# A hinted jump over a guard, first tokens read ahead of weights, and later tables, in a kernel of two attention and two gated layers

## The chip, the core and the metric

The kernel runs on one NeuronCore of a Trainium2 chip. The core has five engines, each with a queue of instructions of its own that it works off in order: TensorE (PE) multiplies matrices, VectorE (DVE), ScalarE (ACT) and GpSimd (POOL) work on rows of numbers, and SyncE (SP) mostly issues transfers (DMAs). They wait for one another through semaphores. On-chip data lie in a buffer of 128 partitions; products are summed in eight banks of a second memory, PSUM. The metric is the device time of one execution in microseconds (us), as a median of several runs; lower is better.

## What is computed

A residual stream x of 2048 tokens with 448 features goes through attention, a gated MLP, the same attention and the same MLP again, with a layer norm ahead of each. The attention has 16 heads of 28 features and no mask.

```python
B, S, D, H = 1, 2048, 448, 16            # F = 1792
def _A_ref(x, wqkv, wo):
    qkv = (x @ wqkv).reshape(B, S, 3, H, Dh).transpose(2, 0, 3, 1, 4)
    q, k, v = qkv[0], qkv[1], qkv[2]
    p = softmax(einsum("bhqd,bhkd->bhqk", q, k) * Dh ** -0.5)
    o = einsum("bhqk,bhkd->bhqd", p, v)
    return o.transpose(0, 2, 1, 3).reshape(B, S, D) @ wo
def _B_ref(x, w_gate, w_up, w_down):
    return (sigmoid(x @ w_gate) * (x @ w_up)) @ w_down

x = x + _A_ref(layernorm(x), A_wqkv, A_wo)
x = x + _B_ref(layernorm(x), B_w_gate, B_w_up, B_w_down)
x = x + _A_ref(layernorm(x), A_wqkv, A_wo)
x = x + _B_ref(layernorm(x), B_w_gate, B_w_up, B_w_down)
```

All of it is in float32. The kernel keeps that accuracy with half-precision products: a number is split into a high and a low float16 part, and three products (high by high, high by low, low by high) stand for one.

## The kernel before

**Order.** The program is written out by hand and not rescheduled: each engine runs its instructions in the order in which the Python code issues them. Each layer has four stages: `project` (q, k and v of all tokens), `attend`, `out_project`, `gated`. Tokens go in four blocks of 512 (`NB`), a block in four tiles of 128 (`TB`).

**The start (L1409 to L1444).** SP issues the reads: `wq.read(0)`, the 448 columns of q's weights (three transfers in `load_rows`: 384 rows, and the last 64 rows twice), then the first four token tiles, one transfer each, then k's weights, the next four tiles, v's weights, the other eight tiles. PE runs fourteen products on zeros (`keep_busy`, L243), which compute nothing that is used, to keep its clock up. ACT adds up the squares of the weights (`measure`, L541); PE sums them over partitions (`size`, L546); DVE makes a power of two of the sum (`powers`, L228 and L230); ACT writes the high half of the scaled weights (`high_cols`, L213) and DVE the low half (`low_cols`, L216). For the tokens, DVE takes the statistics of a tile (`stats`, L430 and L431), POOL makes one over the root of the variance (L433, L435), DVE scales the tile (`scale`, L278), PE turns it (`turn`, L443), and ACT and DVE copy it out of PSUM as high and low parts (`turned_high` L461, `turned_low` L468). POOL's first instructions build constants, among them `ind`, a table of ones that adds up the features of a head, whose last cast DVE makes (L182), and the rows of units that it writes to memory (`unit_scr`).

**`project` (L614).** `qk(b, blk, fill, before)` makes seven tiles of 128 columns of q and k for a block: eleven products each (`by_features`, L492), then ACT copies the high part and squares it (L658, L661), DVE makes the low part and a maximum (L659, L663), and SP writes both to memory (L666). Three tiles later PE adds the squares up for each head (L637, L640, into `qnorm` and `knorm`). In the first block the steps of `along` stand between the tiles and prepare the weights that come later: `measure(1)`, `size(1)`, the halves of k's weights, `measure(2)`, `size(2)`, and v's two halves. `fill[i]` is done behind tile i: for the first block the statistics of the second block's tiles (`b1.norm`) and their scaling (`scaled`). `vals(b, ...)` makes a block's values tile by tile, eleven products of 448 columns each (L514 to L519), and does `after[j]` behind the products of tile j; `fin`, returned by `qk`, adds up the last three tiles' squares and takes their maximum.

**The guard (L796).** The norms bound every score. `worst_of_heads` makes a flag of the bound, each engine loads it into a register (L795), and `tc.If(loose > 0)` runs `true_maxima` for all 16 heads where the bound is too loose: 1,040 products and as many weight loads for PE, in each layer. With these inputs the flag is 0 and every engine jumps over that code. Behind the jump stand the transfers of the first heads' operands and guard rows, the values of the last block's third tile, and the attention.

**`attend` (L1004).** A unit is a block of 128 keys by 512 queries of a head: 1,024 units in a layer. PE makes its scores (L1032), ACT takes the exponential of three units at a time (L1047), PE multiplies them with the values (L1083). Some units are set aside (`ASIDE`): their exponential is made on DVE, in ten instructions (`score_aside`, L1049 to L1067). `FEW` says how many a head sets aside in layer 0; it has 14 characters, and heads beyond it take two; in layer 1 every head takes three. Along with layer 0's attention, DVE and POOL prepare the other weights (`Prepare`). `finish` (L1112) ends a head with a transpose of its sum on DVE.

## Time and profile before

| what | value |
|---|---|
| median of 3 runs | 1936.16 us (1935.15 to 1939.42) |
| the profiled execution | 1937.4 us, span 1935.5 us |
| TensorE busy | 1919.4 us |
| ScalarE busy | 1313.4 us |
| VectorE busy | 1237.3 us |
| GpSimd busy | 164.3 us |
| mean granted TensorE clock | 0.998 |

The span runs from the first to the last instruction of the execution. In it layer 0 has its projection until about 119 us, its attention until 579, its output projection and MLP until about 990; layer 1 has the same with attention from 1080 to 1531. "Busy" counts the time in which an engine has an instruction at work; a product at half clock counts as busy for as long as it lasts. In a timeline each line has the start, the duration, the engine, the line of the code and the operation; behind it, in brackets, how long the engine was idle before it and what released it. The suffix "q" on an engine (PEq) means its sequencer, which fetches and issues the instructions. In the table of windows, each engine's busy time has its count of instructions behind it; then come the granted clock (1.00 is full), the share of the transfer engines' time, and GB/s.

### The profile page before, as it was taken

The page shows a single profiled execution, that of the slowest core. Times are in us where ns is not written, and L with a number is a line of the kernel's source. Part 1 is how long each engine was busy: PE and PEld are TensorE (multiplying, and loading weights), DVE is VectorE, ACT ScalarE, POOL GpSimd, SP SyncE. Part 2 cuts the span into 40 slices and gives each one's busy share as a digit, 9 for nine tenths or more (in the row PEclk, how much of TensorE's full clock was granted, in tenths as well). Part 3 has the DMA queues.
Part 4 walks back from the last instruction along what each step waited for, and adds up shares of the span by engine and source line. Part 5 has one row for each costly group of instructions (what it writes and reads, how often), then busy time and mean ns, then how long its engine had stood idle before and what let it go on. Part 6 is the DMA issues. An engine that isn't in the chain of part 4 may idle for free. (4 is left out here: it accounts for less than half of the span.)

```text
span 1935.5 us, 53590 instructions
## 1 busy us (share of the span) xinstructions
PE 1919.4 (99%) x23405; PEld 1240.8 (64%) x23405; DVE 1237.3 (64%) x2329; ACT 1313.4 (68%) x1573; POOL 164.3 (8%) x307
## 2 busy tenths in 40 slices
PE   9999999999999999999999999999999999999999
PEld 4445555555556777777754576666655577777776
DVE  7638878788655555555574477787778664655543
ACT  5559999999993343443445799999999644343432
POOL 2013322211001000000000000000000000000000
PEclk9999999999999999999999999999999999999999
DMA  5565664424216313242344321122111243333310
GB/s 172 162 203 151 186 199 123 123 84 130 63 62 242 107 69 107 71 132 81 99 117 131 94 51 37 40 51 51 38 39 65 100 171 117 107 111 103 111 46 20
DMA packets 90519, 201.53 MB, mean 104 GB/s; under 512 B 10814, under 2 KB 58014, under 8 KB 90144
## 3 DMA queue, kind: packets, MB, share of 16 engines
q1 hardware_dynamic: 65664, 111.02, 19.4%
q0 software_dynamic: 17776, 83.51, 13.0%
q8 instruction: 188, 3.08, 0.7%
q10 hardware_dynamic: 6832, 3.44, 0.6%
q14 instruction: 59, 0.48, 0.1%
HBM read 142.61 MB, written 47.98 MB: 98 GB/s over the span
## 5 line engine op out<-in xcount | busy, mean ns | idle before, releaser
L1047 ACT ACTIVATE prob_s<-sc 128x1536 f32<-128x1536 f32 x659 | 890.7, 1495 | 13.9 <-PE sc L1032 10.0
L1083 PE MATMUL acc<-prob_s,val_s 128*32 128x256 f32 (+3 forms) x7748 | 569.8, 383 | 0.0
L1032 PE MATMUL sc<-qp_s 114*32 114x512 f16 x7896 | 554.4, 379 | 3.2 <-issue 2.2
L507 PEld LDWEIGHTS <-gu_s 128*128 128x128 f16 x4368 | 426.8, 98 | 61.1 <-issue 1.3
L1032 PEld LDWEIGHTS <-qp_s 114*32 114x32 f16 x8192 | 268.8, 96 | 214.9 <-issue 101.1
L1083 PEld LDWEIGHTS acc<-prob_s,val_s 128*32 128x32 f32 x7748 | 272.0, 110 | 143.6 <-issue 12.0
L1336 DVE TENSOR_TENSOR one_q<-side,one_q 128x512 f32<-128x512 f32 x112 | 71.9, 683 | 298.4 <-PE side L507 298.4
L507 PE MATMUL chain<-xwide_s,gu_s 128*128 128x256 f16 x2016 | 247.6, 273 | 0.6 <-ACT one_q L1320 0.5
L1320 ACT COPY one_q<-chain 128x256 f32<-128x256 f32 x224 | 82.9, 372 | 205.9 <-PE chain L507 199.1
L1063 DVE SCALAR_TENSOR_TENSOR power_q<-power_q,expo_q 128x512 f32<-128x512 f32 x222 | 153.6, 692 | 7.6
L1289 PE MATMUL dnp<-dn_s,hhl_q 128*128 128x448 f16 x448 | 158.0, 353 | 0.0
L1290 PE MATMUL dnp<-dn_s,hhl_q 128*128 128x448 f16 x448 | 158.0, 353 | 0.0
L1291 PE MATMUL dnp<-dn_s,hhl_q 128*128 128x448 f16 x448 | 158.0, 353 | 0.0
L507 PE MATMUL side<-xshort_s,gu_s 128*128 128x256 f16 x1120 | 141.0, 273 | 0.0
L492 PE MATMUL qkp<-xhl_s,wqk_s 128*128 128x512 f16 x616 | 138.0, 379 | 0.8 <-DVE wqk_s L216 0.7
L1112 DVE STREAM_TRANSPOSE oturned_q<-acc 128x512 f32<-128x512 f32 x32 | 22.9, 716 | 143.5 <-PE acc L1083 143.4
L492 PEld LDWEIGHTS <-wqk_s 128*128 128x128 f16 x616 | 60.1, 98 | 70.4 <-DVE wqk_s L216 1.2
L507 PE MATMUL side<-xwide_s,gu_s 128*128 128x256 f16 x672 | 91.7, 273 | 0.0
L1320 ACT COPY two_q<-chain 128x256 f32<-128x256 f32 x112 | 41.7, 372 | 67.5 <-PE chain L507 67.5
L1083 PE MATMUL acc<-power_q,val_s 128*32 128x128 f32 (+3 forms) x276 | 86.3, 394 | 0.0
L1347 ACT ACTIVATE one_q<-one_q 128x512 f32<-128x512 f32 x56 | 35.3, 630 | 59.4 <-DVE one_q L1336 59.4
L1057 DVE TENSOR_SCALAR expo_q<-aside,base 128x512 f32<-128x512 f32 x74 | 55.4, 748 | 30.8 <-PE aside L1032 30.5
(186 smaller groups left out, 2076.7 us busy)
## 6 DMA issues: line engine op xcount, KB each, us to landing
gu_s<-gu_parts POOLq DMA_DIRECT2D x56, 800.0 KB, 4.8
qp_s<-qk_scr SPq DMA_DIRECT2D x96, 224.0 KB
gu_s<-gu_parts SPq DMA_DIRECT2D x20, 800.0 KB
qk_scr<-qkhl_q SPq DMA_DIRECT2D x56, 256.0 KB
gu_parts<-pack_s POOLq DMA_DIRECT2D x14, 800.0 KB, 3.8
xraw_s<-xt_scr SPq DMA_DIRECT2D x12, 768.0 KB
xt_scr<-xs_s SPq DMA_DIRECT2D x34, 224.0 KB
qp_s<-qk_scr SPq DMA_DIRECT2D x64, 112.0 KB
```

Of the source, the lines that this page charges most:

```text
L492: nc.tensor.matmul(pm, w, x, start=(i == 0), stop=(i == len(terms) - 1))
L507: nc.tensor.matmul(pm, a, x, start=(first and i == 0), stop=(i == len(terms) - 1), skip_group_check=True)
L1032: nc.tensor.matmul(ps[32 * j:32 * j + 32, :], hd.k[:, keys], hd.q[:, qb * W:(qb + 1) * W], start=True, stop=True, tile_position=(0, 32 * j))
L1047: nc.scalar.activation(prob[:, 0:n, :], ps[:, 0:n, :], AF.Exp, scale=exp_scale)
L1057: nc.vector.tensor_scalar(y, ps, base2[:, 0:1], -126.0, op0=ALU.mult, op1=ALU.max)
L1063: nc.vector.scalar_tensor_tensor(p, p, c[k], y, op0=ALU.add, op1=ALU.mult)
L1083: nc.tensor.matmul(acc[qb * VC:(qb + 1) * VC, s], v[:, kc % TB, h, :], probs[c * NB + qb][:, s], start=(kc == 0 and a == 0), stop=(kc == N ...
L1289: nc.tensor.matmul(pm, hl[:, 0, s], dw[:, 0, :], start=begin, stop=False)
L1290: nc.tensor.matmul(pm, hl[:, 0, s], dw[:, 1, :], start=False, stop=False)
L1291: nc.tensor.matmul(pm, hl[:, 1, s], dw[:, 0, :], start=False, stop=end)
L1320: nc.scalar.copy(to, pm)
L1336: nc.vector.tensor_tensor(one[m], side[m], one[m], op=ALU.add)
```

## The change

Four things are changed.

1. A hint on PE, "likely taken", is given for the branch of the guard: for layer 0 as the program's first PE instruction, for layer 1 in a new else block of layer 0's guard. In the built program each is one instruction of PE, `BranchPrefetchHint`.
2. At the start the four token tiles are read ahead of q's weights, whose rows come in four transfers instead of three, and whose squares are added up in two parts. Eight products on zeros instead of fourteen are made, and one fewer between the tiles. The sum of squares is taken behind the scaling of the fourth tile, and the larger high part of q's weights (columns 128 to 448) behind the copies of the turned tokens.
3. POOL's table `ind` and the unit rows are made after the first block's statistics, with the cast on POOL instead of DVE. The second block's statistics are taken behind tiles 2 and 3 instead of 0 and 2, its scaling behind tile 5 instead of 4, and in layer 0 `fin` of the second block is done behind the third value tile instead of the second.
4. `FEW` gets two characters more: heads 14 and 15 of layer 0 set three units aside instead of two.

```diff
@@ -61,7 +61,7 @@
 
 
 ASIDE = {1: ((6, 15, 1),), 2: ((4, 10, 3), (9, 15, 1)), 3: ((4, 9, 3), (8, 13, 1), (12, 15, 2))}
-FEW = "22211212121212"
+FEW = "2221121212121233"
 
 N_SLOTS = 19
 N_QUART = 12
@@ -149,6 +149,7 @@
 
     ones = cpool.tile([P, P], F32, name="ones")
     sums = cpool.tile([P, 7], F32, name="sums")
+    rest = cpool.tile([P, 1], F32, name="rest")
     size = cpool.tile([P, 7], F32, name="size")
     pw = cpool.tile([P, 7], I32, name="pw")
     up = cpool.tile([P, 7], F32, name="up")
@@ -168,30 +169,34 @@
     nc.gpsimd.memset(nhalf, -0.5)
     nc.gpsimd.memset(ones, 1.0)
     nc.gpsimd.memset(half, 0.5)
-
-    nc.gpsimd.memset(ind_f, 1.0)
-    for j in range(2):
-        v = ind_f[:, 4 * j:4 * j + 4, :]
-        off = -64 * j
-        nc.gpsimd.affine_select(out=v, in_=v, compare_op=ALU.is_ge, fill=0.0, base=off,
-                                pattern=[[P, 4], [-DH, H]], channel_multiplier=1)
-        nc.gpsimd.affine_select(out=v, in_=v, compare_op=ALU.is_ge, fill=0.0,
-                                base=DH - 1 - off, pattern=[[-P, 4], [DH, H]],
-                                channel_multiplier=-1)
-    nc.gpsimd.memset(ind[:, 8:, :], 0.0)
-    nc.vector.tensor_copy(ind[:, 0:8, :], ind_f)
-    qrt.put(ind_f)
     unit_scr = dpool.tile([2, S], F16, name="unit_scr")
-    units = big.get("units", [2, S], F16)
-    nc.gpsimd.memset(units, UNIT)
-    nc.gpsimd.dma_start(unit_scr, units)
-    big.put(units)
-
-
-    def load_rows(dst, src, c0, n, queue=nc.sync):
-
-        queue.dma_start(dst[:, 0:3, :],
-                        src[0:384, c0:c0 + n].rearrange("(s p) n -> p s n", p=P))
+
+    def tables():
+
+
+        nc.gpsimd.memset(ind_f, 1.0)
+        for j in range(2):
+            v = ind_f[:, 4 * j:4 * j + 4, :]
+            off = -64 * j
+            nc.gpsimd.affine_select(out=v, in_=v, compare_op=ALU.is_ge, fill=0.0, base=off,
+                                    pattern=[[P, 4], [-DH, H]], channel_multiplier=1)
+            nc.gpsimd.affine_select(out=v, in_=v, compare_op=ALU.is_ge, fill=0.0,
+                                    base=DH - 1 - off, pattern=[[-P, 4], [DH, H]],
+                                    channel_multiplier=-1)
+        nc.gpsimd.memset(ind[:, 8:, :], 0.0)
+        nc.gpsimd.tensor_copy(ind[:, 0:8, :], ind_f)
+        qrt.put(ind_f)
+        units = big.get("units", [2, S], F16)
+        nc.gpsimd.memset(units, UNIT)
+        nc.gpsimd.dma_start(unit_scr, units)
+        big.put(units)
+
+
+    def load_rows(dst, src, c0, n, queue=nc.sync, parted=False):
+
+        for a, b in ((0, 2), (2, 3)) if parted else ((0, 3),):
+            queue.dma_start(dst[:, a:b, :],
+                            src[a * P:b * P, c0:c0 + n].rearrange("(s p) n -> p s n", p=P))
         queue.dma_start(dst[0:64, 3, :], src[384:448, c0:c0 + n])
         queue.dma_start(dst[64:128, 3, :], src[384:448, c0:c0 + n])
 
@@ -534,16 +539,21 @@
 
         def read(self, j):
             self.raw.append(big.get("wraw", [P, 4, D]))
-            load_rows(self.raw[j], wqkv, j * D, D)
+            load_rows(self.raw[j], wqkv, j * D, D, parted=(j == 0))
 
         def measure(self, j):
+
             junk = big.get("junk", [P, 4, D], BF16)
-            nc.scalar.activation(junk, self.raw[j], AF.Square, accum_out=sums[:, j:j + 1])
+            for s, to in (((slice(0, 2), sums[:, 0:1]), (slice(2, 4), rest)) if j == 0 else
+                          ((slice(0, 4), sums[:, j:j + 1]),)):
+                nc.scalar.activation(junk[:, s], self.raw[j][:, s], AF.Square, accum_out=to)
             big.put(junk)
 
         def size(self, j):
             pb = bank(7 if j else 3, "sums")
-            nc.tensor.matmul(pb[:, 0:1], ones, sums[:, j:j + 1], start=True, stop=True)
+            nc.tensor.matmul(pb[:, 0:1], ones, sums[:, j:j + 1], start=True, stop=(j > 0))
+            if j == 0:
+                nc.tensor.matmul(pb[:, 0:1], ones, rest, start=False, stop=True)
             powers(j, 1, pb[:, 0:1])
 
         def high_cols(self, j, c0, c1):
@@ -604,6 +614,11 @@
     exp_scale = nc.scalar.alloc_register("exp_scale")
     base2 = cpool.tile([P, 1], F32, name="base2")
     gate_scale = nc.scalar.alloc_register("gate_scale")
+
+    def expect_jump(layer):
+
+        tc.mark_branch_hint_location(f"loose{layer}", hint="LikelyTaken",
+                                     engines=[mybir.EngineType.PE])
 
     def run_fill(fill, n=1):
         for _ in range(n):
@@ -731,7 +746,7 @@
                 b1.turned_high()
                 b1.turned_low()
 
-            fill = [lambda: b1.norm([0, 1]), idle, lambda: b1.norm([2, 3]), idle, scaled]
+            fill = [idle, idle, lambda: b1.norm([0, 1]), lambda: b1.norm([2, 3]), idle, scaled]
             along_values = {0: lambda: (b1.parts(), turned([0, 1])),
                             1: lambda: (turned([2, 3]), big.put(b1.xn)),
                             2: lambda: (fin(), b2.norm()),
@@ -750,7 +765,7 @@
         else:
             fill = [idle, lambda: b2.ready(0, 1), lambda: b2.ready(2, 3), b3.store]
         fin = qk(1, b1, fill, None)
-        vals(1, b1, {0: b3.gather, 1: fin})
+        vals(1, b1, {0: b3.gather, 2 if layer == 0 else 1: fin})
         fin = qk(2, b2, [idle, lambda: b3.ready(0, 1), lambda: b3.ready(2, 3)], None)
         fin = qk(3, blks[3], [], fin)
         if layer > 0:
@@ -793,9 +808,12 @@
         nc.scalar.activation(warm, warm, AF.Exp)
         vals(3, blks[3], {}, range(2))
         loose = nc.values_load(flag[0:1, 0:1], min_val=0, max_val=1)
-        with tc.If(loose > 0):
+        with tc.If(loose > 0, label=f"loose{layer}") as loosely:
             for h in range(H):
                 true_maxima(h)
+        if layer == 0:
+            with loosely.Else():
+                expect_jump(1)
         heads[0].load_guard()
         heads[1].load()
         heads[1].load_guard()
@@ -1016,7 +1034,7 @@
         heads_aside = [0]
         for h in range(H):
             few = FEW if layer == 0 else ""
-            n = int(few[h]) if h < len(few) else 3 if layer > 0 else 2
+            n = int(few[h]) if few else 3
             for at, kc, qb in ASIDE[n]:
                 side[(h * NT + at) * NB] = (h * NT + kc) * NB + qb
             heads_aside.append(heads_aside[-1] + n)
@@ -1407,35 +1425,39 @@
 
 
     new_banks()
+    expect_jump(0)
     wq = WeightsQKV()
     wq.tiles()
     first = Block(0)
     begun = [first]
-    wq.read(0)
     for t in range(TB):
         load_x(t, 1)
+    wq.read(0)
     wq.read(1)
     load_x(TB, TB)
     wq.read(2)
     load_x(2 * TB, 2 * TB)
-    keep_busy(14)
+    keep_busy(8)
     wq.measure(0)
     first.begin()
     first.turn_banks(4, range(4))
     first.parts()
     first.stats(0)
     first.stats(1)
-    wq.size(0)
-    wq.high_cols(0, 0, P)
-    wq.high_cols(0, P, D)
     for t in range(TB):
         first.scale(t)
+        if t == TB - 1:
+            wq.size(0)
         first.turn(t)
-        keep_busy()
+        if t < TB - 1:
+            keep_busy()
         if t + 2 < TB:
             first.stats(t + 2)
+    tables()
+    wq.high_cols(0, 0, P)
     big.put(first.xn)
     first.turned_high()
+    wq.high_cols(0, P, D)
     wq.low_cols(0, 0, P)
     first.turned_low()
     keep_busy()
```

## The prediction

> **What bounds the kernel now.** I read the page first, then TensorE's (PE's) own waits, then the two places where they lie: the guard's jump in each layer and the first 45 us.
>
> ```profile
> PE 1919.4 (99%) x23405; PEld 1240.8 (64%) x23405; DVE 1237.3 (64%) x2329; ACT 1313.4 (68%) x1573; POOL 164.3 (8%) x307
> ...
> q8 instruction: 188, 3.08, 0.7%
> ```
>
> PE is busy for 99% of the span, so an edit gains only where it closes one of PE's few gaps, and "busy" hides stretches at half clock. The queue q8 brings instructions: 3.08 MB / 188 = 16.4 KB a packet, and 46,810 products and weight loads / 188 = some 250 of them in each. The view of waits for PE lists its gaps by releaser (us in total, times, longest):
>
> ```profile
> PE vp L517 <- PEq L796: 1.5, 2, 0.9
> PE sums L546 <- ACT junk_s L541: 1.5, 1, 1.5
> ...
> PE knorm L640 <- DVE sq_q L663: 0.8, 1, 0.8
> PE qkp L492 <- DVE wqk_s L216: 0.7, 1, 0.7
> ```
>
> L796 is the `If` of the guard. The view of that line has the branch on each engine:
>
> ```profile
> L796 DVEq COMPARE_BRANCH  x2: 68/70/72, 116.2 to 1076.1; - x2
> ...
> L796 PEldq COMPARE_BRANCH  x2: 3625/3645/3665, 116.4 to 1076.3; - x2
> ```
>
> PE needs 3.65 us for a branch that takes DVE 0.07 (DVE's own wait for code stands behind it: its next instruction is at 119.1, with nothing on the path). PE's is issued at 116.4, while products in PE's queue last until 119.2. The windows around the first one (busy time, count, then granted clock) show that the loss goes on after it:
>
> ```profile
> 116.00:119.20 3.20, 3.20 (x18) 1.00 0.06 15
> 119.20:120.20 1.00, 0.13 (x1) 1.00 0.88 221
> 120.20:123.00 2.80, 2.78 (x17) 1.00 0.96 222
> 123.00:125.20 2.20, 0.00 (x0) 1.00 0.94 249
> 125.20:126.70 1.50, 1.48 (x20) 1.00 1.03 296
> 126.70:130.20 3.50, 3.50 (x11) 0.51 1.07 252
> ```
>
> One us is lost to the jump, 2.2 more at 123, and then 3.4 us run at half clock: eleven products (`vals`) 0.37 apart instead of 0.19. The stop at 123 waits for no engine. The trace's q8 packets explain it: the jump issued at 116.38 is followed by a packet at 117.39 to 118.72 and PE goes on at 120.04, 1.32 later; the next packet is 122.61 to 123.96 and PE goes on at 125.22, 1.26 later. From the built program, 38 PE instructions lie between the jump's target and the stop. So PE waits twice for code: for the block with the target, and, as the target stands near that block's end, for the next one. In layer 1 the target stands some 90 instructions ahead of a block's end and only the first wait is seen. The timeline of ScalarE (ACT) gives what it costs, first exponentials of layer 0, then of layer 1:
>
> ```profile
> 125.86 2.79 ACT L1047 ACTIVATE prob_s<-sc 128x1536 f32<-128x1536 f32 x2 [5.95 <-PE sc L1032]
> 131.16 4.14 ACT L1047 ACTIVATE prob_s<-sc 128x1536 f32<-128x1536 f32 x3 [2.50 <-PE sc L1032]
> 1083.14 2.79 ACT L1047 ACTIVATE prob_s<-sc 128x1536 f32<-128x1536 f32 x2 [3.14 <-DMA qp_s<-qk_scr]
> 1086.74 4.14 ACT L1047 ACTIVATE prob_s<-sc 128x1536 f32<-128x1536 f32 x3 [0.80 <-PE sc L1032]
> ```
>
> The last product ahead of the jump starts at 118.98 and at 1079.07; the third group of exponentials 12.18 and 7.67 after it. Layer 0 loses 4.5 us to layer 1 there.
>
> The start, from the timeline:
>
> ```profile
> 7.00 1.70 ACT L541 ACTIVATE junk_s<-wraw_s 128x1792 bf16<-128x1792 f32 x1 [4.70 <-DMA wraw_s<-in_A_wqkv_dram]
> 7.36 0.63 DVE L430 BATCH_NORM_STATS2 st<-x 128x6 f32<-128x448 f32 x1 [2.23 <-DMA x<-in_A_x_dram]
> 14.32 1.56 ACT L461 CAST xhl_s<-turn 128x512 f16<-128x512 f32 x3 [2.64 <-PE turn L443]
> 15.10 5.46 PE L492 MATMUL qkp<-xhl_s,wqk_s 128*128 128x512 f16 x22
> 32.35 2.08 DVE L216 SCALAR_TENSOR_TENSOR wv_s<-wraw_s,up,wv_s 128x1792 f16<-128x1792 f32 x1
> ```
>
> Weights and first tokens land together near 7. The weights are ready for products at 10.3, the tokens, through statistics, scaling and turning, only at 14.8. Later VectorE (DVE) decides: PE's second value product stands at 34.48, behind the low half of wv, which ends at 34.34.
>
> **The change, part by part.**
>
> 1. *Start.* SP issues x's four reads ahead of wraw. 290 KB had landed by 3.5 before, so x's first 224 KB land near 3.6, and the chain that began at 7.36 begins 3.7 us earlier; its last scaling ends at 9.5. The first weights take the place in line of x's fourth tile, whose last piece landed at 9.65 (14 of 16 by 8.5): I take 8.6, bounds 7 and 9.65. The one read more (wraw in four parts) costs SP one issue, 0.45; what follows in its queue is wanted only from 14.7. Then, by rows: second half of the measuring 1.0 (half of 1.70 plus 0.19), sum and powers 0.9, first high part 0.65, first copy 0.5, and 0.3 later, as before, the first product starts: at 12.0, 3.1 earlier. Eight `keep_busy` products at 0.44 end at 4.8, so PE's clock may be halved somewhere in 8 to 15, as it was from 10.7 to 14.1; a half-clock product (0.43) still fits between copies that come every 0.52 to 0.63, hence 0.1 to 0.9 us.
> Part of the 3.1 is given back. On DVE the block statistics move behind tiles 2 and 3, 1.5 us each, still ahead of `powers(2)`, so ACT's high half of wv waits for them; and the four scalings (1.7), which filled DVE's time until that half was ready, now come after wv's low half. Laying DVE's and ACT's rows end to end in the new order, with waits of 0.2, 1.0, 0.8, 1.3 and 1.1 us for ACT, wv's low half ends near 32.1 (2.2 earlier), and the turned block waits 0.5 for the late scalings. Net gain at the end of the first values: 1.9, bounds -0.6 (weights at 9.65 and two half-clock stretches) and 2.7. Pool's tables (about 5 us with the cast taken from DVE, whose row there was 1.92 because it overlapped Pool's fill) run from 9 to 14.5 in Pool's queue, ahead of the value fills (2.2) and of statistics wanted at 26; the table is first read by the norm products of tile 3, near 20. The unit rows' write goes out ten us later and is read at 108. Hidden.
> 2. *`fin` one value tile later:* the 0.8 at `knorm` goes, covered by 2.08 us of value products. Bounds 0 and 0.8.
> 3. *The hints.* Each is one PE instruction: the first ahead of PE's wait for DVE until 1.25, the second in the else block while queued products run. Nearest row, PE's semaphore instructions: 0.05; free in both places. No row shows what a hint does. Bounds: nothing, or both code waits vanish. For the upper one the target's block must be there at 116.4; the block after it, asked for then, would by the lag of 2.5 us seen twice between going on and the next packet start near 119 and be usable near 121.6, when score products begin. Layer 0 then starts like layer 1 without its jump: 4.5 + 0.8 = 5.3. Layer 1's gap, 1079.07 to 1080.09 less one product (0.19), is 0.8. I take the upper end: the branch stands at a fixed place, and the nearest rows for a branch whose target is loaded, ACT's and POOL's, which skip nothing, are 0.05. Guard rows (issued 117.6, landed by 119.2) are in time for scores at 121.3; behind them the ACT queue waits only for PE.
> [...]
> 4. *A third unit aside in heads 14 and 15 of layer 0.* Two units leave ACT (2 x 0.45 at most, and the last odd group), ten DVE instructions of 0.7 come on in each head, where DVE is busy for 15.6 of 27.9 us. By the transposes that end each head, heads 4 to 14 take 27.97 each in layer 0, and 27.76 with three units in layer 1; heads 14 and 15 together 53.1 and 53.3. I take 0.2 for both, bounds -0.3 and 1.0. Products on PE stay as many.
>
> Sum: 1.9 + 0.8 + 5.3 + 0.8 + 0.2 = 9.0. The profiled execution took 1937.4 (span 1935.5 and 1.9 around it), so 1928.4; it lies 1.2 above the median of the runs, 1936.16, and there it gives 1927.
>
> **Rivals.**
> - *The hint does nothing* (armed 116 and 960 us ahead, lost by the time it is wanted). For it: nothing in this trace shows a branch prefetched. Against: the instruction exists for exactly a branch like this. Only parts 1, 2 and 4 are left: 2.9, so 1933.2.
> - *Only the jump is covered,* and the second block is still fetched late: 1.0 + 0.8 from part 3, so 4.7 in all: 1931.4.
> - *The hint takes the fetch's look-ahead.* If an armed hint makes the fetch bring the target in place of the next block in line, every block on the way comes on demand. Place: all of layer 0 after the jump, 93 blocks from 118 to 1076. Price: 1.0 us each where the queue covers the rest, as at the jump, up to 2.6, as at 122.6: +93 to +240 us, 2020 or more. It decides from nine such blocks at 1.0, which eat the whole gain. For it: 3.65 us is what a block on demand costs. Against: a hint that did so would be of no use to anyone.
>
> **How the numbers follow.** My forecast 0.62, its own range 1925 to 1930.5 (the bounds above); nothing 0.24; jump alone 0.08; look-ahead 0.04; 0.02 for the rest. The range runs from 1924.5 to 1933.7, to take in the case without effect. About 0.2% (3.9 us, below 1932.3) can be told from no change: faster 0.62 + 0.07 + 0.04 (a lucky start without hint) = 0.73, same 0.20, slower 0.07.
>
> **What would show it.** Right: PE's COMPARE_BRANCH under 0.3 us twice, no PE gap at 119 and 123 and no half clock after it, third exponentials some 7 us after the last product ahead of the jump; first L492 product near 12.0 and PE waiting over a us for wv's low half; no wait at `knorm`. Wrong: a branch of 3.6 us again, or first products at 14 because weights land after 10.

## The result and the profile after

| | before | after |
|---|---|---|
| median of 11 runs each, side by side | 1937.45 us (1934.8 to 1939.42) | 1932.37 us (1930.96 to 1934.72) |
| the profiled execution | 1937.4, span 1935.5 | 1932.95, span 1930.8 |

The ratio is 0.9976, 95% interval 0.9967 to 0.9985: the change saves 4.6 us (2.9 to 6.4; the medians differ by 5.1), where 9.0 were forecast. 1932.37 lies inside the range on record (1924.5 to 1933.7), but between the times of the first two rivals (a hint that does nothing, 1933.2, and a hint that covers the jump alone, 1931.4); as a saving, 4.6 is what the second of them gives (4.7). So the time can't tell whether the hint works, and that is the first thing to read. The view of the guard's line, now L811 (each row: engine, instruction, count, shortest/median/longest ns):

```profile
L811 DVEq COMPARE_BRANCH  x2: 68/70/72, 116.8 to 1072.7; - x2
L811 PEldq COMPARE_BRANCH  x2: 367/373/379, 117.1 to 1072.9; - x2
```

It does: 3.65 us became 0.37 in both layers. The windows around layer 0's jump (length, then busy time and count of PE, PEld, DVE, ACT and POOL, then granted clock, share of the transfer engines, GB/s):

```profile
119.50:120.70 1.20, 0.57 (x4) 0.22 (x3) 0.00 (x0) 0.54 (x1) 0.00 (x0) 1.00 0.46 58
120.70:123.00 2.30, 2.30 (x15) 1.03 (x18) 0.08 (x1) 0.00 (x0) 2.27 (x4) 1.00 0.95 234
123.00:125.20 2.20, 2.20 (x30) 0.95 (x23) 0.54 (x1) 1.51 (x2) 0.47 (x1) 1.00 1.02 256
125.20:126.70 1.50, 1.50 (x15) 0.65 (x17) 0.19 (x1) 1.29 (x1) 0.00 (x0) 1.00 1.03 312
```

The stop of 2.2 us at 123 is gone (q8's first packet behind the jump, issued at 117.1, begins at 118.2 and ends at 119.3; before, packets began at 117.4 and at 122.6, the second just ahead of the stop), and so is the half clock behind it. A gap at the jump itself is left: 119.66 to 120.64 from product to product, 0.98 us against 1.23 before. So the 3.3 us by which layer 0's branch is shorter took only 0.25 us off the stop at that jump; most of the gain lies behind it. The first exponentials of layer 0, then of layer 1:

```profile
123.69 2.79 ACT L1065 ACTIVATE prob_s<-sc 128x1536 f32<-128x1536 f32 x2 [3.10 <-PE sc L1050]
127.29 5.48 ACT L1065 ACTIVATE prob_s<-sc 128x1536 f32<-128x1536 f32 x4 [0.80 <-PE sc L1050]
1079.19 2.79 ACT L1065 ACTIVATE prob_s<-sc 128x1536 f32<-128x1536 f32 x2 [2.62 <-DMA qp_s<-qk_scr]
1082.79 8.17 ACT L1065 ACTIVATE prob_s<-sc 128x1536 f32<-128x1536 f32 x6 [0.81 <-PE sc L1050]
```

The last product ahead of the jump starts at 119.66 and at 1075.63, so the third group comes 7.63 and 7.16 us after it (12.18 and 7.67 before): 4.55 and 0.51 us gained. But 119.66 is 0.68 *later* than before, although `fin` no longer waits. The loss is in the start (lines from the timelines of ACT and PE):

```profile
9.66 0.95 ACT L549 ACTIVATE junk_s<-wraw_s 128x896 bf16<-128x896 f32 x1 [7.37 <-DMA wraw_s<-in_A_wqkv_dram]
11.40 0.95 ACT L549 ACTIVATE junk_s<-wraw_s 128x896 bf16<-128x896 f32 x1 [0.69 <-DMA wraw_s<-in_A_wqkv_dram]
12.49 0.58 PE L556 MATMUL sums<-rest,ones 128*128 128x1 f32 x2 [1.29 <-ACT junk_s L549]
12.94 1.09 PE L448 MATMUL turn<-ident,xn_s 128*128 128x128 f32 x4
14.74 7.10 PE L497 MATMUL qkp<-xhl_s,wqk_s 128*128 128x512 f16 x22 [0.28 <-ACT xhl_s L466]
21.82 4.91 PE L497 MATMUL qkp<-xhl_s,wqk_s 128*128 128x512 f16 x22
36.11 0.35 PE L523 MATMUL vp<-wv_s,xhl_s 128*128 128x448 f16 x1 [1.08 <-DVE wv_s L221]
```

The weights landed at 11.29, not at 8.6. The fourth transposition of the tokens, whose scaling ended at 10.12, stands behind the sum of squares in PE's queue and so waited for the weights too (12.94). The first product came at 14.74 instead of the 12.0 forecast (15.10 before), the first 22 took 7.10 us instead of 5.46, and the second value product started at 36.11, 1.63 us later than before. In the traces PE's clock is granted for stretches of 3.41 us or a multiple of it (half clock for 3.41 from 10.69 and from 126.74 before, for 6.83 from 12.26 after). Windows cut at the edges of these stretches show what made the 7.10:

```profile
5.43:8.85 3.42, 1.74 (x10) 0.97 (x10) 2.70 (x7) 0.00 (x0) 1.83 (x5) 1.00 1.05 311
8.85:12.26 3.41, 1.22 (x7) 0.78 (x7) 0.55 (x2) 1.91 (x4) 3.11 (x10) 1.00 1.11 258
12.26:15.67 3.41, 2.90 (x9) 1.55 (x10) 1.73 (x5) 2.36 (x7) 2.93 (x8) 0.50 0.99 306
15.67:19.09 3.42, 3.42 (x10) 1.14 (x9) 3.36 (x4) 3.40 (x4) 0.60 (x3) 0.50 1.13 323
```

PE works for 1.22 us of the stretch 8.85 to 12.26, waiting for the weights; the next two stretches run at half clock.

### The profile page after: what moved, and what is told of

Its sections match the earlier page's. It is cut to its first block, busy times and chain, and to the rows that moved or that the text cites. A ratio compares the mean times of both kernels' runs of the same rounds, so it can differ in the third digit from the quotient of the medians.

```text
span 1930.8 us, 53585 instructions
## 1 busy us (share of the span) xinstructions
PE 1915.8 (99%) x23392; PEld 1327.5 (69%) x23392; DVE 1248.2 (65%) x2348; ACT 1314.0 (68%) x1574; POOL 164.5 (9%) x308
## 5 line engine op out<-in xcount | busy, mean ns | idle before, releaser
L1101 PE MATMUL acc<-prob_s,val_s 128*32 128x256 f32 (+3 forms) x7732 | 591.6, 383 | 0.0
L1050 PE MATMUL sc<-qp_s 114*32 114x512 f16 x7888 | 575.8, 379 | 0.9 <-ACT prob_s L1065 0.9
L1050 PEld LDWEIGHTS <-qp_s 114*32 114x32 f16 x8192 | 315.8, 95 | 173.0 <-issue 80.0
L1101 PEld LDWEIGHTS acc<-prob_s,val_s 128*32 128x32 f32 x7732 | 321.5, 110 | 96.2 <-issue 7.0
L1081 DVE SCALAR_TENSOR_TENSOR power_q<-power_q,expo_q 128x512 f32<-128x512 f32 x228 | 157.8, 692 | 7.8
```

What stands on the lines that cost most here:

```text
L1050: nc.tensor.matmul(ps[32 * j:32 * j + 32, :], hd.k[:, keys], hd.q[:, qb * W:(qb + 1) * W], start=True, stop=True, tile_position=(0, 32 * j))
L1081: nc.vector.scalar_tensor_tensor(p, p, c[k], y, op0=ALU.add, op1=ALU.mult)
L1101: nc.tensor.matmul(acc[qb * VC:(qb + 1) * VC, s], v[:, kc % TB, h, :], probs[c * NB + qb][:, s], start=(kc == 0 and a == 0), stop=(kc == N ...
```

## The experiments

All times are medians beside runs of the kernel before on the same chip. In the traces the starts of four things on one path are compared: the first projection product, the 23rd, DVE's low half of wv, and the last product ahead of layer 0's jump. "Landing" is the last piece of the first 1.72 MB (q's weights, whose last rows are read twice and counted once here, and the first four token tiles).

| kernel | landing | first product | 23rd | wv low | last ahead of jump | ratio to before, 95% |
|---|---|---|---|---|---|---|
| before | 9.65 | 15.10 | 20.53 | 32.35 | 118.98 | 1 |
| after | 11.29 | 14.74 | 21.82 | 33.98 | 119.66 | 0.9976 [0.9967, 0.9985] |
| e1 hints only | 8.96 | 14.63 | 20.06 | 31.88 | 118.57 | 0.9978 [0.9969, 0.9987] |
| e2 no hints | 10.45 | 13.86 | 21.11 | 33.26 | 118.94 | 0.9991 [0.9982, 1.0] |
| e3 old start | 9.07 | 15.76 | 20.79 | 32.94 | 118.62 | 0.9974 [0.9964, 0.9984] |
| e4 warm | 11.50 | 14.75 | 20.52 | 32.67 | 118.35 | 0.997 [0.9959, 0.998] |
| e5 whole, warm | 10.53 | 14.60 | 21.51 | 33.65 | 119.34 | 0.9981 [0.9972, 0.999] |
| e6 old start, warm | 8.67 | 14.31 | 19.75 | 31.89 | 117.57 | 0.997 [0.9958, 0.9982] |
| e7 powers | 11.39 | 14.64 | 20.41 | 31.53 | 117.21 | 0.9962 [0.9948, 0.9976] |
| e8 best | 11.07 | 13.85 | 19.20 | 30.32 | 116.00 | 0.9963 [0.9949, 0.9976] |
| e9 old start, powers | 8.93 | 14.36 | 19.79 | 30.91 | 116.60 | 0.9962 [0.9948, 0.9975] |
| e11 best again | 11.44 | 14.23 | 19.59 | 30.70 | 116.38 | 0.9963 [0.9949, 0.9976] |
| e13 best, third time | 11.16 | 13.94 | 19.30 | 30.42 | 116.11 | 0.9957 [0.9943, 0.997] |

### What the hints pay, and what the rest pays (e1, e2)

e1 is the kernel before with these lines only; e2 is the changed kernel without them.

```diff
+        tc.mark_branch_hint_location(f"loose{layer}", hint="LikelyTaken",
+                                     engines=[mybir.EngineType.PE])
...
-        with tc.If(loose > 0):
+        with tc.If(loose > 0, label=f"loose{layer}") as loosely:
...
+        if layer == 0:
+            with loosely.Else():
+                expect_jump(1)
...
+    expect_jump(0)
```

> The kernel before with nothing but the two fetch hints of part 3. My account of the two traces: the hints pay 4.55 us in layer 0 (third exponential after the last product ahead of the jump: 12.18 to 7.63) and 0.5 in layer 1, so this kernel should be 5.0 us under the kernel before (ratio 0.9974) and as fast as the changed kernel, whose other parts then sum to about nothing. Rival: the hints pay only what the whole change paid beyond its start (about 3 us, 0.9985), because later waits take the rest back; then the start of the changed kernel gained. In the trace I look for a branch of 0.37 us twice and a start like that of the kernel before (first projection product at 15.1).

> The changed kernel without the two hints, everything else kept. By my account the rest of the change is start -1.5, the sum fin +0.8, heads 14 and 15 +0.1: 0.6 us slower than the kernel before (ratio 1.0003, range 0.9995 to 1.001). If the start had gained the 1.9 us of the forecast it would be 2.8 us faster (0.9986). In the trace: branch of 3.6 us twice, last product ahead of the jump at 119.7 as in the changed kernel.

e1 took 1932.72 us against 1937.23: 4.5 us less, and within 0.4 us of the changed kernel. So the hints alone make nearly the whole effect, and the other parts sum to about nothing beside them. e2 took 1935.54: 1.7 less, where 0.6 more was expected; its interval reaches 1.0, so this is hardly told from nothing. Its exponentials show why the parts don't simply add:

```profile
125.71 2.79 ACT L1062 ACTIVATE prob_s<-sc 128x1536 f32<-128x1536 f32 x2 [5.84 <-PE sc L1047]
129.32 2.79 ACT L1062 ACTIVATE prob_s<-sc 128x1536 f32<-128x1536 f32 x2 [0.82 <-PE sc L1047]
```

The third group comes 10.38 us after the last product (118.94), not 12.18, although both code waits are there (gaps of 1.45 and 2.28 us). What is missing is the half clock. In the kernel before, the stretches fell so that one held most of the second stop:

```profile
119.91:123.33 3.42, 2.78 (x17) 1.12 (x18) 0.62 (x1) 0.00 (x1) 2.45 (x4) 1.00 0.96 230
123.33:126.74 3.41, 1.52 (x20) 0.68 (x20) 0.00 (x0) 0.88 (x1) 0.30 (x1) 1.00 0.99 277
126.74:130.15 3.41, 3.41 (x11) 1.18 (x8) 0.00 (x0) 1.92 (x2) 0.00 (x0) 0.50 1.04 245
```

In e2 they fell at 120.94, 124.36 and 127.77, with 2.45 and 2.48 us of work, and the clock stayed. Where the stretches begin differs from one execution to the next (119.91 and 120.94 here), so the price of the same two stops is 2.75 us in one (10.38 - 7.63) and 4.55 in the other.

### What of the start costs the time (e3, e4, e6)

e3 puts the old start under the new hints, `fin`, heads and places of the second block's statistics. e4 is the changed kernel with eight busy products after the third transposition; e6 is e3 with 20 busy products for 14 and five after the sum of squares.

```diff
-            keep_busy()
+            keep_busy(8 if t == TB - 2 else 1)
```

> The changed kernel with the start of the kernel before (weights read first and in one piece, 14 busy products, Pool's tables first, square sum and rounding ahead of the first transpositions); hints, fin and heads 14 and 15 kept. My account: the new start costs 1.5 us, so this is 1.5 us faster than the changed kernel, 6.5 under the kernel before (ratio 0.9966), last product ahead of the jump at 118.2. If the new start gained 1.9 it is 1.9 slower than the changed kernel (0.9986).

> The changed kernel with 8 busy products in place of 1 after the third transposition, so that TensorE works in the 3.4 us stretch 8.85 to 12.26 after which the trace shows half clock until 19.09. Theory A: the half clock costs the first 22 products 7.10 - 5.46 = 1.64 us and passes on: 1.6 us faster than the changed kernel (ratio to before 0.9968), clock 1.0 throughout, second tile's products at 20.2. Theory B: the late weights set the end of the start through VectorE's low half of the value weights (36.06): the first 22 products get 5.46 us but the second value product still starts at 35 to 36, and the time stays within 0.5 us of the changed kernel's (0.9973 to 0.9977).

> The kernel of e3_old_start with 20 busy products in place of 14 and 5 after the sum of squares, so that TensorE is not idle around 7.4 to 10.1 us and the half clock (two windows in e3, one in the kernel before) stays away. Theory A (half clock is what the start loses): 22 projection products in 4.7 to 4.9 us from the first, which starts at 14 to 14.6; last product ahead of the jump about 1.6 us earlier than in e3 (118.62), at 117.0, and the time 1.0 to 1.6 us under e3: ratio 0.9967. Theory B (late weights and VectorE's queue set it): first product as in e3 or e1, the second value product still at 34 to 35 and the time equal to e3 within 0.4 us.

e3 (1931.82, ratio 0.9974) can't be told from the changed kernel, where 1.5 us were expected, and its first product came at 15.76: in this execution the stretches fell at 5.81, 9.22 and 12.63, and the last two of them ran at half clock.

e4 took 1931.16 and e6 1930.62, each with a ratio of 0.9970 and clock 1.0 throughout its trace. The last product ahead of the jump is 1.31 us earlier in e4 than in the changed kernel, and 1.05 earlier in e6 than in e3. So by the traces the half clock at the start costs somewhat over a us and passes on to the end (theory A), less than the 1.64 of the first 22 products, since in e4 the tenth product waits 0.18 for VectorE and the first 22 take 5.77. The times alone don't decide between the two theories: 0.9970 lies between 0.9968 and 0.9973. The clocks of all executions agree with the traces: the changed kernel's eleven have a mean granted clock of 0.997 to 0.999, e4's eight 0.999 or 1.0, and the five each of e7, e8 and e9 1.0. With the clock held, tokens first (e4) and weights first (e6) have the same ratio.

### The cut of the first weights (e5)

e5 is e4 with the first weights read as before, 384 rows in one transfer, and squared whole.

```diff
-            load_rows(self.raw[j], wqkv, j * D, D, parted=(j == 0))
+            load_rows(self.raw[j], wqkv, j * D, D)
```

> The kernel of e4_warm with the first weights read in the three transfers of the kernel before (384 rows, then two tails) and squared whole; first tokens still ahead of them. Question: why do the same 1.72 MB land at 11.3 to 11.5 in the new order (10.45 once) and at 9.0 to 9.65 in the old one. Theory A: the cut into smaller transfers does it, since SP needs 0.4 to 0.6 us for each issue; then the last weight lands by 10 and the first product starts near 14.0. Theory B: the order itself does it; the last weight lands at 10.5 to 11.5, and because the square (1.9 us instead of 0.95 after the last landing) is now in one piece, the first product starts near 15.5, 0.8 us later than in e4_warm: ratio to before 0.9974 against 0.997.

The landing, 10.53, is theory B's; the first product, 14.60, is neither's: the earlier landing made up for the longer square. PE stood still for 1.82 us while it waited, the stretch 11.77 to 15.19 held 1.54 us of work, and the next ran at half clock in spite of the eight busy products; 1933.12 us.

### The late statistics (e7, e9)

```diff
-            fill = [idle, idle, lambda: b1.norm([0, 1]), lambda: b1.norm([2, 3]), idle, scaled]
+            fill = [idle, idle, lambda: b1.norm([0, 1]), idle, lambda: b1.norm([2, 3]), scaled]
```

> The kernel of e4_warm with the statistics of block 1's last two token tiles two places later, behind the power of two of the value weights. In e4 that power waits behind them on VectorE: sum at 28.2, power at 30.50, ScalarE's half 30.85 to 32.64, VectorE's half to 34.75, second value product at 34.81 after 1.08 us of waiting. Theory: the power comes at 29.1, the halves 1.3 us earlier, TensorE's wait of 1.08 is gone, and the last product ahead of the jump is 1.0 us earlier: 0.9965 against 0.997. Rival: the wait moves to block 1 (its statistics, scaling and transpositions are later now), a wait of about 1 us for xn or for the transposed tokens takes its place, and the time stays.

> The kernel of e6_old_warm (weights read first, TensorE kept busy) with the edit of e7: statistics of block 1's last two tiles behind the power of the value weights. Theory: the wait of 1.07 us for the low half of the value weights goes as it did in e7 (from 1.08 to under 0.2), and the time is 1.0 us under e6: 5.1 to 7.2 us under the kernel before (0.9965), so that the order of the reads is worth at most the 0.5 us between this and e7. Rival: with the weights first VectorE is free later and the wait stays at 0.5 or more: time as e6.

DVE's timeline of e4, then of e7 (the power of two of wv, and wv's low half):

```profile
30.50 0.13 DVE L233 TENSOR_SCALAR pw<-sums 128x1 int32<-128x1 int32 x1
32.67 2.08 DVE L221 SCALAR_TENSOR_TENSOR wv_s<-wraw_s,up,wv_s 128x1792 f16<-128x1792 f32 x1 [1.06 <-ACT wv_s L218]
```
```profile
28.91 0.15 DVE L233 TENSOR_SCALAR pw<-sums 128x1 int32<-128x1 int32 x1
31.53 2.08 DVE L221 SCALAR_TENSOR_TENSOR wv_s<-wraw_s,up,wv_s 128x1792 f16<-128x1792 f32 x1
```

The sum was ready at 28.2 in e4; the power stood behind two statistics in DVE's queue. In e7 PE's wait for wv's low half is no longer in its list, the last product ahead of the jump comes 1.14 us earlier, and the median is 1929.51 (ratio 0.9962 against 0.9970 of e4, with intervals that overlap). e9 does the same to the old start: 0.97 us earlier than e6 at the jump, 1929.57. No new wait of PE stands between the start and the jump in either trace.

### The order of the first transpositions (e8, e11)

```diff
-        if t == TB - 1:
-            wq.size(0)
         first.turn(t)
-        if t < TB - 1:
-            keep_busy(8 if t == TB - 2 else 1)
+        keep_busy((1, 1, 5, 4)[t])
...
+    first.high(0, nc.vector)
+    first.high(1, nc.vector)
+    wq.measure(0, 1)
+    first.high(2)
+    wq.size(0)
...
```

> The kernel of e4_warm with the fourth transposition ahead of the sum of squares on TensorE, two of the four copies of the transposed tokens on VectorE (idle from 10.6 to 13.1 in e4) and one on ScalarE behind the last square, so that they don't follow the weights' rounding. Theory: first product at 14.25 instead of 14.75, no wait of 0.18 at the tenth one, VectorE's queue 1.5 us shorter behind 14 us; 0.5 to 0.7 us faster than e4_warm (0.9967 against 0.997), the wait for the low half of the value weights as it was. Rival: ScalarE's and VectorE's order around 11 to 14 delays the powers and the first product comes at 14.7 or later: no gain.

The kernel that ran is e7's with this edit, not e4's as the text on record says, so it is read against e7. The first product comes at 13.85 (14.64 in e7), the last ahead of the jump 1.21 us earlier in the trace, the median is the same 1929.51. e11 repeats it beside others:

> The kernel of e8_best1 once more, beside the three others on one chip: ratio 0.9963, 7.2 us under the kernel before. All parts of it were measured apart: hints, e4's busy products, e7's order of VectorE, e8's order of the first transpositions.

1929.35 against 1937.61, the same ratio of 0.9963; its weights landed later (11.44), and with them its first product. At the jump e11 is still 0.83 us ahead of e7, whose weights landed as late (11.39). In the times, beside e7 and e9, the gain of this edit can't be told from nothing.

### The hints without the other losses (e10, e12)

e10 and e12 leave out both hints, or the second one, of e8.

> The kernel of e8_best1 without the two hints. What the hints pay is the difference to e11_best_again on the same chip. Theory from the traces: 2.75 us in layer 0 where no half clock follows the stall (e2: third exponential 10.38 after the last product, with the hint 7.63), 4.55 where it does (before: 12.18), and 0.3 to 0.5 in layer 1: 3.1 to 5.0, likely 4. Rival (the forecast's terms): 6.1. In the trace: branches of 3.6, and the third exponential either 10.4 (clock 1.0) or 12.2 (half clock right behind) after the last product.

> The kernel of e8_best1 with the first hint alone, the one for layer 1 left out. Theory: the gap of layer 1's jump goes from 0.50 back to 0.8 to 1.0 us and the branch to 3.4 to 3.6, so 0.3 to 0.5 us slower than e11_best_again. Forecast on record: 0.8. Rival: layer 1's jump is covered by the products queued ahead of it: no difference.

e10: 1933.94 us, so the hints pay 4.6 by the medians (3.5 by the ratios, 0.9981 and 0.9963). Its branches took 3.83 and 3.85 us, and its stretches fell badly:

```profile
114.29:117.70 3.41, 2.37 (x13) 1.10 (x12) 0.00 (x0) 0.54 (x1) 0.67 (x1) 1.00 0.66 156
117.70:121.11 3.41, 1.55 (x12) 0.52 (x13) 0.62 (x1) 0.00 (x0) 2.08 (x4) 1.00 0.98 225
121.11:124.52 3.41, 3.41 (x27) 1.22 (x20) 0.00 (x0) 2.32 (x2) 0.00 (x0) 0.50 1.03 252
```

The third group of exponentials came 11.92 us after the last product (7.63 in e11): 4.29 in layer 0. e12: the branch of layer 1 takes 3.79 us again, the gap at the jump is 1.18 instead of 0.50, and the third group comes 7.83 after the last product instead of 7.15. That is 0.68; the medians differ by 0.45 and the ratio is 0.9961, which these runs can't tell from nothing.

### Does the hint hold the first reads back? (e13 to e18)

In the two kernels with no hint at the start (e2, e10) the weights landed at 10.45 and 9.71, in those with one at 10.53 to 11.50. e13 (from e8) and e14 (from the changed kernel) were to give the hint behind the first block's values, e15 (from e8) at 4.9 us.

```diff
-    expect_jump(0)
...
         vals(0, blks[0], along_values)
+        if layer == 0:
+            expect_jump(0)
```

> The kernel of e8_best1 with the first hint given after the first block's values (about 37 us) instead of at 0.9 us. Theory H (the hint's fetch holds back the first reads): the last piece of the first weights lands at 9.7 to 10.4 instead of 11.07 and 11.44, the slowest of its 16 parts no more than 0.8 us behind the twelfth instead of 0.9 to 2.1, first product at 12.9 to 13.4 instead of 13.85 and 14.23, and the time 0.5 to 1.0 us under e8 (0.9958 to 0.996); the branch still takes 0.37. Theory O (the order of the reads and chance): landing at 10.5 to 11.5, first product at 13.8 to 14.3, time as e8 (0.9963).

> The changed kernel with the first hint given after the first block's values, nothing else altered. Theory H: the last weights land at 9.7 to 10.5 instead of 11.29, first product at 13.3 to 13.9 instead of 14.74; half clock as the stretches of 3.4 us happen to fall; 0.5 to 1.0 us faster than the changed kernel (0.997 to 0.9972 against 0.9976). Theory O: landing 10.5 to 11.5, time as the changed kernel.

> The kernel of e8_best1 with the first hint behind the eight busy products, at 4.9 us, in the middle of the first reads. Theory H: late parts again, but only in pieces that land after 5 us: the last weights at 11 or later, first product at 13.8 to 14.3, time as e8 (0.9963). Theory O: no difference to e13.

These three failed as experiments: in their traces the hint instruction still runs at 0.885 us, as in e8. In all three it went to the head of its straight stretch of code, wherever the call stood. So e13 and e15 repeat e8 (1928.97 and 1929.51; landing 11.16 and 11.04) and e14 repeats the changed kernel (1933.0, ratio 0.9977; landing 10.40). e16 is e4, e17 is e7 and e18 is e8, each without hints, with one execution each.

> The kernel of e4_warm without the two hints, one look at its trace: when does the last piece of the first weights land? Theory H (the hint holds the reads back): at 10.5 or earlier, as in e2 and e10. Theory O (the order of the reads and chance; no packet of instructions is recorded between 0 and 20 us, with the hint or without): anywhere between 9.7 and 11.5, and in at least one of the three looks of this call later than 10.6. Time about 1935.5 (the 4.6 us of the hints above e4).

> The kernel of e7_powers without the two hints, one look: the same question. Theory H: last piece of the first weights at 10.5 or earlier. Theory O: between 9.7 and 11.5. Time about 1934.2.

> The kernel of e10_best_none once more, one look: the same question. Theory H: the last piece of the first weights at 10.5 or earlier, 9.71 again or near it. Theory O: between 9.7 and 11.5. Time about 1934.

The weights landed at 11.09, 11.84 and 10.36. 11.84 is later than in any trace with the hint: theory H falls. Over the fifteen traces with tokens read first the landing is 9.71 to 11.84, over the five with weights first 8.67 to 9.65, for the same bytes. In the former the twelfth of the 16 parts of the last weight transfer is in by 9.0 to 10.2, and the others straggle by up to 2.8 us. The cut alone doesn't do it (e5), and the hint doesn't. What is left is the order of the reads, which no run separates from the rest of the new start. The windows show one thing more: from 3 to 5 us the transfer engines move 361 to 381 GB/s in the five traces with weights first and 204 to 262 in the fifteen with tokens first, and over the first 9.65 us 252 to 258 and 213 to 234. So with the new start the rate is lower, besides the other place in line; why, these runs don't show.

The times (1937.43, 1937.02, 1934.5) are of that one execution, beside one of the kernel before that took 1934.46; they decide nothing. e16 and e17 took 2 to 3 us more than expected, and their traces have a half clock at the start in spite of the busy products: e16 from 7.9 to 11.4, behind a stretch with 1.73 us of work, e17 from 16.2 to 19.6. So eight busy products don't exclude the half clock: with them it came at the start in three of five traces (e5, e16, e17; not in e4 and e7), without them, tokens first, in three of three (the changed kernel, e2, e14). All three executions have it behind the second code wait too (from 124.0, 125.4 and 122.5), and the third group of exponentials 11.94, 12.30 and 12.37 after the last product.

The best program that ran is that of e8, e11, e13 and e15: 1928.97 to 1929.51 in four sets of runs, ratios 0.9957 to 0.9963, some 3 us under the changed kernel.

## Why the prediction was right and wrong, by its steps

**What bounds the kernel** was read rightly: PE's gaps at the start and at the jump. e1 closes the stops behind the jump and e7 one at the start, and the time follows by 4.5 and some 1.5 us (1.1 for e7 in the trace).

**1, the start, failed: 1.9 us of gain forecast, 1.6 of loss in the trace.** The step that failed is "the first weights take the place in line of x's fourth tile ... I take 8.6, bounds 7 and 9.65". They landed at 11.29: equal bytes in another order came 1.6 us later than the upper bound. The rest of that sum held: with 11.29 in place of 8.6 its terms give 14.7 for the first product, and 14.74 was measured. Of the 4.0 us by which the second value product is behind the forecast (36.1 for 32.1), 2.7 stand at the first product already. The other 1.3 came behind it. In detail:
- The forecast let the tokens' chain end at 9.5 by itself. The last scaling did end at 10.1, but its transposition stands behind the weights' sum on PE, a queue that the prediction did not read there. By the sum above this cost nothing that shows in the changed kernel; taking the transposition ahead, with two copies moved, gave 0.4 at the first product (e11 against e7, with weights that landed equally late).
- The half clock was priced at 0.1 to 0.9 us, argued from copies that would be the limit. PE was the limit: the first 22 products took 1.64 us longer, and e4 shows 1.31 us of it at the jump.
- PE waits 1.08 us for wv's low half, as forecast ("over a us"), but up to 36.1 and not to 32.1: with PE late too, this wait is a loss and no rest of a gain. The new place of the statistics makes it: e1, with the old place, waits 0.2 there, e3 and e6, with the old start and the new place, 1.1, and in e7 the wait is gone.

With clock and DVE's queue mended, tokens first (e7) and weights first (e9) have the same ratio, 0.9962: reading the tokens ahead is worth nothing that these runs can tell.

**2, `fin`, was right.** e1 still has the wait and no other part of the change; its list of PE's waits says

```profile
PE knorm L645 <- DVE sq_q L668: 0.9, 1, 0.9
```

and the changed kernel's list has no such row. From the second value product to the last product ahead of the jump 84.5 us pass in the kernel before and in e1, and 83.5 in the changed kernel and in every other trace, all of which have `fin` moved. So of the 1.63 us lost at the start 0.95 come back here, which leaves the 0.68.

**3, the hints: the mechanism was right, the size was not.** Both code waits vanish, and a packet of q8 begins at 118.2, at the jump; that it brings the block for which PE waited at 123 before is the author's reading. Forecast 6.1; measured 4.5 (e1) and 4.6 (e10) by the medians, 5.1 from trace to trace. Two terms were too large. "Layer 0 then starts like layer 1 without its jump: 4.5 + 0.8": the third group still comes 7.63 after the last product and not 6.9, because behind the jump PE now waits for ScalarE's copy out of the accumulator that the next value tile needs, which used to lie inside the code wait (in the trace before that copy ended at 119.9 and PE went on at 120.2; after, 120.6 and 120.6):

```profile
PE vp L522 <- ACT val_s L706: 0.6, 1, 0.6
```

VectorE (DVE) comes close behind. It got no hint and stands 2.8 to 3.7 us behind its own branch in layer 0, in all twenty traces. The prediction found "nothing on the path" there, but with PE's hint DVE frees PE's next weight load only 0.1 to 0.7 us before that copy ends, and in e9 it ends the stop itself:

```profile
PE vp L523 <- DVEq L807: 0.7, 1, 0.7
```

No run gives DVE a hint. And 1.8 of the 4.5 was half clock (12.18 less the 10.38 of e2), which comes when the stretches fall so: in five of the six traces without a hint in layer 0 (11.92 to 12.37), not in e2 (10.38). Layer 1 gave 0.51 of the 0.8 in this trace; over all traces without its hint it is 0.2 to 0.8 (third group 7.38 to 7.92 after the last product, 7.16 with the hint). The rivals without effect, with the jump alone, and with the look-ahead taken all fall by the branch of 0.37 us, the missing stop at 123 and the 185 packets of q8 (188 before). Without a hint PE's branch takes 3.3 to 3.9 us in every trace, and 0.37 to 0.40 with one.

**4, heads 14 and 15,** was forecast at 0.2: their span is 53.03 us after, 53.11 before and 53.12 in e1, so 0.1.

The trace's sum: 0.7 lost up to the jump, 4.55 gained behind it, 0.4 lost up to layer 1's jump, 0.5 gained there and 0.75 behind it; 4.7 of span, 4.3 less than forecast. Of these 4.3 the start and `fin` make 3.4 (0.7 lost for 2.7 gained) and the hints 1.0 (5.1 for 6.1). That the time still lies inside the range is in part luck: the range was drawn wide enough to hold a hint without effect, and a loss at the start filled that room. The 0.4 and 0.75 are spread over 1,800 us and have no cause that was shown.

## What to carry to other kernels

A known jump over a large block can be announced to PE: here its branch took 0.37 us in place of 3.65, in layer 1 with the hint run 955 us ahead (117.6 for 1072.9). What that saves depends on what else the engine waits for at the jump, other engines' jumps among it (0.6 us for ScalarE's copy in the changed kernel, 0.7 for VectorE's jump in e9); look at the code behind the target too, where most of the gain lay here (4.3 of 4.55 us). When work is put earlier, read every in-order queue on its way for what now stands ahead of it, and don't price a landing by the place in line: here the same bytes came some 2 us later in another order (9.71 to 11.84 for 8.67 to 9.65). Here PE's clock was halved behind stretches in which PE stood idle, and idle products in its waits paid 1.31 us (e4) and 1.05 (e6) at the jump, by the traces.

## What the runs showed of the hardware

- In the first 140 us of the traces, counting stretches that begin inside the span, wherever PE worked for 1.55 us or less of a 3.41 us stretch at full clock (eleven cases, 0.75 to 1.55), the next stretch ran at half clock; with 1.73 to 1.96 it did in three of eight, with 2.0 or more never. At half clock, 2.46 to 3.13 us of work kept it there (four cases), 3.17 and more ended it. Where the stretches start differs between executions (7.27 before, 6.66 in e1, 5.81 in e3), so one program with idle times near these figures has several times: 1934.1 to 1939.7 for the kernel before. Its 75 executions beside e1 to e18 sort by their mean granted clock: 1935.8 us on average at 0.999 (26 of them), 1937.6 at 0.998 (46), 1938.8 at 0.997 (3).
- In these traces the branch takes 0.37 to 0.40 us on PE with a hint, 3.3 to 3.9 without. In the changed kernel no packet of q8 begins near the first hint, at 0.89: the first is at 28.6 (27.7 before, without a hint). Near the jump the packets of q8 begin at 102.9, 118.2 and 123.6 after, at 102.3, 117.4, 122.6 and 130.7 before, one more. What a packet holds no trace shows; that the one at 102.9 brings the target's code, as the one at 117.4 does before, is the author's estimate from this count.
